# The last block of the first FFN and the whole second FFN go into the planner's order; the first units get an order by hand

## The chip, the cores and the metric

The kernel runs on 1 core of one Trainium2 chip. The metric is the device time of one execution in microseconds (us). Matrix products run on TensorE (PE in the profile; PEld is its weight load), elementwise work on VectorE (DVE), ScalarE (ACT) and GpSimd (POOL), and SyncE (SP) issues all transfers of the program.

## The reference

Attention over a window of 64 positions, an FFN with ELU, and a gated FFN on normalized rows, all in float32 on 2304 tokens of width 512:

```python
scores = scale * np.matmul(q, k.transpose(0, 1, 3, 2))     # 4 batches, 8 heads, 576 positions, head_dim 64
mask = (rel >= 0) & (rel < window)                         # rel = query position - key position, window 64
attn = softmax of np.where(mask, scores, -1e9)
x = np.matmul(attn, v), as 2304 rows of 512

h = x @ w_in                                               # 512 x 2048
x = np.where(h > 0, h, np.exp(np.minimum(h, 0)) - 1) @ w_out   # 2048 x 512

xn = x / np.sqrt(np.mean(x * x, axis=-1) + 1e-6) * rms_g
g = xn @ w_gate                                            # 512 x 1536
out = (g * sigmoid(g) * (xn @ w_val)) @ w_out2             # 1536 x 512
```

## The kernel before

**Precision.** A float32 operand is held as a high part (fp32r) and a low part, and each product is three: high times high, low times high, high times low. A weight tile (a "unit", 128 x 512) goes through four steps: POOL moves the top halves (L569, `s1`), DVE joins the halves (L576, `join`), ACT or DVE makes the high part (L587, `s2`), POOL the low part (L592, `s3`). The text calls these steps G, J, H and L, with the number of the weight, as the new code does. There are 32 such units of the first FFN, all made while block 0 runs; they stay in SBUF as the 32 slots of the tag `wu`.

**First stage.** Tokens go in six blocks of 384. For a block, three attention units of 128 tokens: transpositions of keys and queries (T, L371), scores (S, L403), masking and minimum on DVE (M, L424), exponentials on ACT (E, L430), normalization on DVE (N, L436 to L438), transposition of the weights (TP, L455), values (PV, L467), copies between (L384). Then the first FFN: for each of 16 slices of 128 columns a product `in` (12 matmuls, L621), ELU on ACT and DVE (L669 to L678), and a product `out` two slices later (12 matmuls, L696) into four PSUM banks of the tag `y`. The attention of block b+1 runs between the products of block b. Of each block the four `y` banks are copied to SBUF, normalized and stored in DRAM (`xspill`).

**Second stage.** Three superblocks of 768 tokens. A 2 x 2 Strassen-like scheme needs seven products per pair of column slices instead of eight: weight combinations `pu` are made beforehand by POOL and ACT, stored in DRAM (`pspill`, and `ospill` for the output weights, through two staging tiles `stg`), and loaded again; row combinations X are made by DVE. Each of 6 pairs per superblock has 7 x 12 matmuls (L1022), whose results go through `c` tiles (copies L984 on ACT, sums L988 on DVE), the gate (L993 to L1005), and after three pairs the output product (`outs`, L1056).

**What sets the order.** Class `Plan` (from L25) takes steps with a cost per engine, the tiles they read and write, and for loads a time on the transfer queue (`load`). `run` (L161) repeatedly takes the step that can start first, with `tail` (the longest chain behind it) deciding among those within 0.1 us. `could` (L106) gives the earliest time by engine, inputs and free buffers (`LIMITS`, L22). Costs are raised by `MARGIN`: DVE by 1.2, ACT and POOL by 1.1. Every instruction is then tied behind the one before it on its engine. Before, only blocks 0 to 4 (`planned = nblk - 1`, L1097) are planned. Block 5 and the second FFN are written out at the kernel's end in a fixed interleaving (slots, `after()`), and the order of their instructions on each engine is the scheduler's of the tile framework. There `norm_items` (L705) does the normalization with copies `big<-y` at L708 and the final multiplications at L742; `split_out` (L878) stages output weights (L882, L885).

Of the kernel before, what the change touches and what calls it, by code (L numbers as in the profile page):

```python
# [21 lines left out]
LIMITS = dict(w=4, y=4, wu=32, kT=2, qT=1, ks=1, qs=1, vw=2, s=2, st=3, pT=2, e=2, g=3, x0=1, x1=1,  # L22
# [7 lines left out]
class Plan:  # L30
# [4 lines left out]
    WINDOW, PREFER = 0.1, 0.5  # L35
    MARGIN = {"DVE": 1.2, "ACT": 1.1, "POOL": 1.1}
# [4 lines left out]
    def add(self, costs, fn, reads=(), writes=(), load=0.0, rows=128):  # L41
        x = Step()
        x.costs = {e: c * self.MARGIN.get(e, 1.0) for e, c in costs.items()}
        x.fn, x.index, x.load, x.rows = fn, len(self.steps), load, rows
# [24 lines left out]

    def lag(self, a, e):  # L70
        return 0.0 if a == e else 0.22 if a == "PE" else 0.09

    def tails(self):
# [14 lines left out]
        for t in self.users:  # L88
            if t[0] in LIMITS:
                every.setdefault(t[0], []).append(t)  # L90
                if t[0] not in "wy" and (t[0] != "wu" or t[1][0] in ("r", "in", "out")):
                    self.first.setdefault(t[0], []).append(t)
# [7 lines left out]
        self.queued = {t for ts in self.first.values() for t in ts}  # L100
# [5 lines left out]
    def could(self, x, e):  # L106
        t = self.free.get(e, 0.0)
# [8 lines left out]
        for tag, ts in new.items():  # L116
# [6 lines left out]
            ts = ts.intersection(self.queued)  # L123
            for tile in self.first.get(tag, ()) if ts else ():
                if tile not in self.live:
                    if tile not in ts:
                        return None
                    ts.discard(tile)
                    if not ts:
                        break  # L130
# [30 lines left out]
    def run(self):  # L161
# [10 lines left out]
        ready = [x for x in self.steps if not x.deps]  # L172
        while ready:
            per = {}
# [6 lines left out]
            assert per, ("the plan is stuck", [(list(x.costs), x.tiles, x.index) for x in ready], self.used)  # L181
# [9 lines left out]
            self.put(x, e, t)  # L191
            ready.remove(x)
            for y in after[x.index]:
                wait[y.index] -= 1
                if not wait[y.index]:
                    ready.append(y)
        return self.order


@with_exitstack  # L200
def kernel(
# [99 lines left out]
    N0 = BLOCKS1[0] // 128  # L301
    plan = Plan()
# [27 lines left out]
    def load_steps(nm, i, src, t0, n, bufs):  # L330
# [10 lines left out]
        add({"SP": 0.55 * parts}, go, writes=[a_key(nm, i, bufs)], load=1.25)  # L341
# [10 lines left out]
    def attention(u, xt=None, b=0, x=None):  # L352
# [14 lines left out]
        def turn(bkey, nm):  # L367
# [6 lines left out]
            add({"PE": 0.436}, go, reads=[a_key(nm, u, 1)], writes=[bkey])  # L374
# [11 lines left out]
        turn(bk, "ks")  # L386
        turn(bq, "qs")
# [898 lines left out]
```

## Time and the profile before

| | us |
|---|---|
| median of 3 executions | 933.17 |
| lowest, highest | 933.01, 934.4 |
| the profiled execution | 932.11 |
| its span, first to last instruction | 930.3 |
| PE busy in the span | 905.0 |
| DVE, ACT, POOL busy | 566.8, 446.3, 238.2 |
| mean granted clock of TensorE | 0.994 |

How to read it: the profile is of one execution, so stretches and waits are compared with its own 932.11 us. An engine executes its instructions in order; "idle before" is time in which it had nothing running, with what ended that time behind the arrow. PEclk is the granted share of TensorE's 2.4 GHz: 1.00 or 0.50 (1.2 GHz). A busy PE does not say that it ran at its full clock.

### The profile page before, as it was taken

To read this page: it belongs to the slowest core of one execution; us is meant where nothing else is said; L and a number is where in the kernel's file an instruction comes from. 1 tells how busy PE (TensorE), PEld (TensorE's weight loads), DVE (VectorE), ACT (ScalarE), POOL (GpSimd) and SP (SyncE) were. 2 spreads that over 40 slices of the span, in tenths; PEclk is the share of its full clock that TensorE was granted. 3 is DMA by queue.
4 is the path that set the end of the run, shared out by engine and by line. 5 is a ranking of instruction groups with operands and counts; after the bars stand their busy time and mean duration, and the time that the engine had idled before them with its cause. 6 is when DMAs were issued, how large, how long until landed. Compare 5 with 4: busy or idle time off the path is not lost.

```text
span 930.3 us, 16271 instructions
## 1 busy us (share of the span) xinstructions
PE 905.0 (97%) x5916; PEld 855.7 (92%) x5916; DVE 566.8 (61%) x1266; ACT 446.3 (48%) x1131; POOL 238.2 (26%) x281
## 2 busy tenths in 40 slices
PE   6799999999999999999999999999999999999998
PEld 4798999999999999999999888998998998998996
DVE  5889867567655755674876583375460485460561
ACT  5766565666656566565423642441441441441430
POOL 3687803540561453056123113000000000000000
PEclk9899999999999999999999999999999999999999
DMA  9997117543733663554486487936966747847711
GB/s 210 306 318 207 25 24 216 170 137 101 235 131 103 206 198 118 141 178 160 157 281 240 148 318 249 388 142 236 404 232 213 232 138 268 314 136 252 220 49 69
DMA packets 150401, 182.96 MB, mean 197 GB/s; under 512 B 81712, under 2 KB 111408, under 8 KB 150320
## 3 DMA queue, kind: packets, MB, share of 16 engines
q1 hardware_dynamic: 150320, 181.91, 60.3%
q8 instruction: 47, 0.77, 0.4%
q14 instruction: 34, 0.28, 0.1%
HBM read 144.13 MB, written 37.75 MB: 196 GB/s over the span
## 4 chain that ended last, share of the span: by engine, by line
PE 66%; DMA 12%; DVE 11%; POOL 4%; ACT 4%; issue 2%; SPq 0%; POOLq 0%; ACTq 0%; DVEq 0%
PE y L1022 15%; PE w L1022 11%; PE y L1056 11%; PE w L621 10%; PE y L696 10%; PE w L1056 5%; DMA pspill<-stg 4%; DMA ospill<-stg 3%; DVE wm L576 2%; POOL stg L922 1%; PE w L467 1%; DMA big<-in_moe_w_val_dram 1%; DMA ks<-in_k_dram 1%; DMA big<-in_moe_w_gate_dram 1%; PE w L403 1%
## 5 line engine op out<-in xcount | busy, mean ns | idle before, releaser
L696 PE MATMUL y<-g,wu 128*128 128x384 f32 x1152 | 220.2, 340 | 0.6 <-DVE g L678 0.4
L621 PE MATMUL w<-x,wu 128*128 128x384 f32 x1152 | 217.2, 337 | 0.0
L696 PEld LDWEIGHTS y<-g,wu 128*128 128x128 f32 x1152 | 200.2, 189 | 5.1 <-DVE g L678 1.4
L621 PEld LDWEIGHTS w<-x,wu 128*128 128x128 f32 x1152 | 199.2, 188 | 1.9 <-issue 1.0
L1022 PE MATMUL y<-xw,pu 128*128 128x384 f32 x648 | 123.6, 335 | 1.9 <-ACT big L708 1.3
L1022 PEld LDWEIGHTS y<-xw,pu 128*128 128x128 f32 x648 | 113.3, 188 | 3.2 <-ACT big L708 1.6
L988 DVE TENSOR_TENSOR c<-c,w 128x384 f32<-128x384 f32 x72 | 39.7, 551 | 119.1 <-PE w L1022 118.5
L1056 PE MATMUL y<-wu,g 128*128 128x512 f32 x432 | 106.4, 390 | 0.0
L1056 PEld LDWEIGHTS y<-wu,g 128*128 128x128 f32 x432 | 80.9, 188 | 16.1
L569 POOL CAST top<-big 128x512 f16<-128x512 bf16 x36 | 31.6, 879 | 201.4 <-DMA big<-in_moe_w_gate_dram 63.9
L1022 PE MATMUL w<-xw,pu 128*128 128x384 f32 x432 | 82.6, 334 | 0.0
L1022 PEld LDWEIGHTS w<-xw,pu 128*128 128x128 f32 x432 | 75.6, 188 | 0.1
L678 DVE TENSOR_TENSOR g<-e,g 128x384 fp32r<-128x384 f32 x80 | 59.1, 742 | 20.6 <-ACT g L676 19.5
L673 DVE SCALAR_TENSOR_TENSOR e<-e,w 128x384 f32<-128x384 f32 x80 | 43.6, 549 | 38.7 <-ACT e L671 38.4
L984 ACT COPY c<-y 128x384 f32<-128x384 f32 x72 | 34.4, 481 | 65.7 <-PE y L1022 64.7
L669 ACT ACTIVATE e<-w 128x384 f32<-128x384 f32 x80 | 39.0, 488 | 40.3 <-PE w L621 38.0
L1056 PE MATMUL w<-wu,g 128*128 128x512 f32 x216 | 55.9, 390 | 0.0
L1004 ACT CAST g<-e 128x384 fp32r<-128x384 f32 x69 | 34.9, 512 | 41.5 <-DVE e L998 41.5
L430 ACT ACTIVATE s<-s,st 128x128 f32<-128x128 f32 x120 | 46.7, 391 | 9.2 <-DVE st L424 9.1
L993 ACT ACTIVATE e<-c 128x384 f32<-128x384 f32 x54 | 27.5, 524 | 46.7 <-DVE c L988 46.6
L922 POOL TENSOR_TENSOR stg<-wm,stg 128x256 fp32r<-128x256 f32 x48 | 38.4, 800 | 44.8 <-ACT stg L920 44.7
L1056 PEld LDWEIGHTS w<-wu,g 128*128 128x128 f32 x216 | 40.6, 188 | 8.6
(153 smaller groups left out, 1307.7 us busy)
## 6 DMA issues: line engine op xcount, KB each, us to landing
pu<-pspill SPq DMA_DIRECT2D x126, 512.0 KB, 6.7
pspill<-stg SPq DMA_DIRECT2D x84, 256.0 KB, 2.2
wu<-ospill SPq DMA_DIRECT2D x36, 512.0 KB, 5.9
tmp<-in_moe_w_out_dram SPq DMA_DIRECT2D x16, 511.8 KB, 7.3
tmp<-in_moe_w_in_dram SPq DMA_DIRECT2D x16, 511.0 KB, 7.4
vw<-in_v_dram SPq DMA_DIRECT2D x27, 256.0 KB, 3.7
ospill<-stg SPq DMA_DIRECT2D x24, 256.0 KB, 2.5
big<-in_moe_w_out_dram SPq DMA_DIRECT2D x12, 511.8 KB, 7.5
```

Of the source, the lines that this page charges most:

```text
L430: nc.scalar.activation(out=s_()[:, p, :], in_=s_()[:, p, :], func=AF.Exp, scale=-1.0, bias=st_()[:, 0, p, :], accum_out=st_()[:, 1, p, :])
L621: nc.tensor.matmul(pt[:, :n], lhsT=wt[:, a, kk * 128:(kk + 1) * 128], rhs=xs[kk][:, c, :n], start=(i == 0), stop=(i == len(seq) - 1))
L669: add({"ACT": 0.49}, lambda e: nc.scalar.activation(out=et(), in_=ph(), func=AF.Relu, scale=-1.0), reads=[w], writes=[e_])
L673: add({"DVE": 0.56}, lambda e: nc.vector.scalar_tensor_tensor(out=et(), in0=et(), scalar=-1.0, in1=ph(), op0=ALU.add, op1=ALU.max), reads= ...
L678: add({"DVE": 0.68}, lambda e: nc.vector.tensor_tensor(out=gt()[:, 1, :n], in0=et(), in1=gt()[:, 0, :n].bitcast(F32), op=ALU.subtract), re ...
L696: nc.tensor.matmul(py[m][:, :n], lhsT=wt[:, a, m * 128:(m + 1) * 128], rhs=g[:, c, :n], start=(first and i == 0), stop=(last and i == 2))
L922: add({"POOL": 0.76}, lambda e: nc.gpsimd.tensor_tensor(out=tile_()[:, 1, :], in0=src(), in1=tile_()[:, 0, :].bitcast(F32), op=ALU.subtrac ...
L984: nc.scalar.copy(out=t, in_=bank[b, qi][:, :NB])
L988: nc.vector.tensor_tensor(out=t, in0=t, in1=bank[b, qi][:, :NB], op=ALU.add)
L1004: nc.any.tensor_copy(out=g[:, 0, :], in_=e)
L1022: nc.tensor.matmul(bank[key][:, :NB], lhsT=u[:, qi, a, kk * 128:(kk + 1) * 128], rhs=X[j][kk][:, x, :], start=(first and n == 0), stop=(n ...
L1056: nc.tensor.matmul(po[m], lhsT=g[:, a, (m % 3) * 128:(m % 3 + 1) * 128], rhs=w[:, x, :], start=(first and i == 0), stop=(last and i == 2))
```

## The change

- Block 5 and the second FFN become steps of the plan: `norm_items`, `elu`, `split_out` and the slots of the old end go, and `norm_steps` (with `tail=True` for the last block), `in_steps`, `out_steps`, `put_out`, `x_load`, `x_items`, `p_load`, `o_load`, `pair` and `outs` add steps. The scheduler has no order left to choose.
- The first 20 loads (`LOADS`) and the first steps of units 0 to 2 with weights 0 to 5 (`FIRST`) are placed in an order given by hand; the planner continues from there. H of weights 0 to 4 is put on DVE; before, these five were on ACT. In both programs 27 of the 32 H are on ACT and 5 on DVE.
- A load is planned no earlier than 4 us before the planned end of the transfer queue (`AHEAD`).
- `MARGIN` is now 0.92 for PE and 1 for the others; some costs are other numbers (J 0.85 to 1.05, G 0.88 to 1.0, H on DVE 0.75 to 1.0, N 1.6 in block 1). Keys of unit u are transposed only after the scores of unit u-1.
- The matrix products, their operands and their number are the same.

```diff
-    WINDOW, PREFER = 0.1, 0.5
-    MARGIN = {"DVE": 1.2, "ACT": 1.1, "POOL": 1.1}
+    WINDOW, PREFER, AHEAD = 0.1, 0.5, 4.0
+    MARGIN = {"PE": 0.92}
...
     def could(self, x, e):
-        t = self.free.get(e, 0.0)
+        t = max(self.free.get(e, 0.0), self.dma - self.AHEAD if x.load else 0.0)
...
-    def run(self):
+    def run(self, given=()):
...
+        given = [(x, e) for name, e in given for x in self.steps if x.name == name]
+        pos = 0
         while ready:
+            if pos < len(given):
+                x, e = given[pos]
+                pos += 1
+                e = e if e in x.costs else next(iter(x.costs))
+                self.take(x, e, self.could(x, e), ready, wait, after)
+                continue
...
+    LOADS = "ks0 qs0 ks1 qs1 ks2 qs2 vw0 vw1 w0 vw2 vw3 w1 vw4 vw5 w2 w3 w4 w5 w6 w7"
+    FIRST = (
+        "Tk0 Tq0 CK0 CKa0 Tk1 CQ0 S0 CK1 Tq1 M00 E00 Tk2 CKb0 M01 CQ1 N00 CK2 S1 E01 CKb1 TP00 "
...
-    for b in range(planned):
-        n = BLOCKS1[b]
+    for b in range(nblk):
+        n, last = BLOCKS1[b], b == nblk - 1
+        slots = {}
...
+        if last:
+            x_load(0)
+            for j in range(AHEAD2):
+                slots.setdefault(7 + j, []).append(lambda n=j: p_load(0, n))
+            for j in range(F2 // 2):
+                slots.setdefault(6 + j * 10 // (F2 // 2), []).append(lambda j=j: prep_out(j))
+            for j, fn in enumerate(x_items(0)):
+                slots.setdefault(7 + j * 3 // 2, []).append(fn)
...
-    def norm_steps(b, n, tok0):
+    def norm_steps(b, n, tok0, tail=False):
...
...
+        def keep(pos, qi, j):
+            ck, bk = c_key(pos, qi), bank(j, qi)
+            add({"ACT": 0.48}, lambda e: nc.scalar.copy(out=c_of(ck), in_=at(bk)),
+                reads=[bk], writes=[ck])
...
-    for x, e in plan.run():
+    for x, e in plan.run(given):
```

**Where instructions move.** First, SP at the program's start (tmp tiles of keys, queries and values of units 0 to 2 by their DRAM tensors; `in_moe_w` are weights of the first FFN). Before:

```order
L293 DMA tmp_135<-in_k_dram 128x8x64
L293 DMA tmp_137<-in_q_dram 128x8x64
L293 DMA tmp_139<-in_v_dram 64x8x64 x2
L293 DMA tmp_139<-in_v_dram 128x8x64
L293 DMA tmp_135<-in_k_dram 128x8x64
L293 DMA tmp_137<-in_q_dram 128x8x64
L293 DMA tmp_150<-in_v_dram 128x8x64 x2
L293 DMA tmp_163<-in_k_dram 128x8x64
L293 DMA tmp_167<-in_q_dram 128x8x64
L563 DMA tmp_187<-in_moe_w_in_dram 128x4x511
L563 DMA tmp_189<-in_moe_w_in_dram 128x4x511
L293 DMA tmp_194<-in_v_dram 128x8x64 x2
```

After the change:

```order
L307 DMA tmp_135<-in_k_dram 128x8x64
L307 DMA tmp_137<-in_q_dram 128x8x64
L307 DMA tmp_135<-in_k_dram 128x8x64
L307 DMA tmp_137<-in_q_dram 128x8x64
L307 DMA tmp_141<-in_k_dram 128x8x64
L307 DMA tmp_143<-in_q_dram 128x8x64
L307 DMA tmp_145<-in_v_dram 64x8x64 x2
L307 DMA tmp_145<-in_v_dram 128x8x64
L586 DMA tmp_149<-in_moe_w_in_dram 128x4x511
L307 DMA tmp_151<-in_v_dram 128x8x64 x2
L586 DMA tmp_154<-in_moe_w_in_dram 128x4x511
L307 DMA tmp_156<-in_v_dram 128x8x64 x2
```

Keys and queries of all three units now stand ahead of the first values, the first weight ahead of the values of units 1 and 2, and the second weight behind those of unit 1.

Second, ACT at the end of block 5, where its `y` banks are copied (`big<-y`, L708 before, L738 now); `stg<-wm` are staging copies of output weights, `c<-y` the first copies of the second FFN, `x<-xb` row combinations. Before:

```order
L882 CAST stg<-wm 128x256 x2
L841 CAST x_6159<-xb 128x384
L639 ACTIVATE e<-w 128x384
L841 CAST x_6165<-xb 128x384
L882 CAST stg<-wm 128x256
L640 ACTIVATE e<-e 128x384
L882 CAST stg<-wm 128x256 x3
L708 COPY big_6170<-y 128x384
L708 COPY big_6171<-y 128x384
L712 ACTIVATE big_6172<-big_6170 128x384 x2
L882 CAST stg<-wm 128x256 x2
```

After the change:

```order
L863 CAST stg<-wm 128x256
L685 CAST g<-e 128x384
L863 CAST stg<-wm 128x256
L678 ACTIVATE e<-w 128x384
L680 ACTIVATE e<-e 128x384
L821 CAST x_6101<-xb 128x384
L821 CAST x_6122<-xb 128x384 x2
L685 CAST g<-e 128x384
L863 CAST stg<-wm 128x256 x2
L738 COPY big_6163<-y 128x384 x2
L738 COPY big_6175<-y 128x384
```

Before, three staging copies in a row stand right in front of the bank copies, of which ACT does two; now two stand there, and ACT does three of the four.

Third, DVE in the first three pairs, where the normalization of block 5 ends with its multiplications by `g_sb` (L742 before, L763 now), among the sums `c<-c,w` (L988, now L987) that free PSUM banks. Before:

```order
L737 SCALAR_TENSOR_TENSOR big_6172<-e,big_6172 128x384
L998 TENSOR_TENSOR e<-e,y 128x384
L988 TENSOR_TENSOR c<-c,w 128x384
L742 SCALAR_TENSOR_TENSOR big_6170<-big_6170,g_sb,big_6172 128x384 x2
L742 SCALAR_TENSOR_TENSOR big_6171<-big_6171,g_sb,big_6172 128x384 x2
L988 TENSOR_TENSOR c<-c,w 128x384
L1005 TENSOR_TENSOR g<-e,g 128x384
L994 TENSOR_TENSOR e<-e,c 128x384
L988 TENSOR_TENSOR c<-c,y 128x384 x2
L988 TENSOR_TENSOR c<-c,w 128x384
```

After the change:

```order
L759 SCALAR_TENSOR_TENSOR big_6242<-e,big_6242 128x384
L987 TENSOR_TENSOR c<-c,w 128x384
L763 SCALAR_TENSOR_TENSOR big_6163<-big_6163,g_sb,big_6242 128x384
L987 TENSOR_TENSOR c<-c,w 128x384
L991 TENSOR_TENSOR e<-e,c 128x384
L987 TENSOR_TENSOR c<-c,y 128x384 x2
L991 TENSOR_TENSOR e<-e,c 128x384
L987 TENSOR_TENSOR c<-c,w 128x384
L991 TENSOR_TENSOR e<-e,c 128x384
L987 TENSOR_TENSOR c<-c,w 128x384
```

The four multiplications stood together ahead of a sum; now one stands between two sums, and none of the other three among the next seven rows.

## Rows read from the trace of the kernel before

**Rows 1.** The page, part 1: busy time, share of the span, instructions.
```profile
PE 905.0 (97%) x5916; PEld 855.7 (92%) x5916; DVE 566.8 (61%) x1266; ACT 446.3 (48%) x1131; POOL 238.2 (26%) x281
```

**Rows 2.** Busy time by stage: stretch, length, engines' busy us, PEclk, DMA share, GB/s.
```profile
32.80:43.05 10.25, 7.71 (x52) 7.10 (x44) 9.34 (x30) 7.71 (x26) 9.40 (x9) 1.00 1.02 269
43.05:46.46 3.41, 3.22 (x13) 3.23 (x13) 2.79 (x5) 2.01 (x4) 1.21 (x3) 0.50 1.04 362
46.46:120.00 73.54, 72.14 (x573) 68.65 (x572) 65.14 (x122) 44.61 (x111) 59.50 (x49) 1.00 0.61 174
120.00:500.00 380.00, 377.99 (x2800) 365.41 (x2799) 246.61 (x603) 221.68 (x602) 135.72 (x167) 1.00 0.54 167
500.00:538.00 38.00, 36.01 (x202) 34.47 (x201) 25.27 (x49) 18.01 (x41) 7.79 (x10) 1.00 0.39 126
538.00:541.40 3.40, 1.46 (x9) 1.14 (x7) 3.40 (x8) 0.13 (x1) 0.00 (x0) 1.00 0.69 170
541.40:544.80 3.40, 3.19 (x10) 3.19 (x11) 3.23 (x8) 1.85 (x4) 0.00 (x0) 0.50 1.00 378
560.00:920.00 360.00, 360.00 (x1887) 335.68 (x1885) 174.09 (x339) 121.49 (x255) 8.14 (x11) 1.00 0.63 222
```

**Rows 3.** Timeline of ACT, 9 to 34 us: start, length, instruction, idle before.
```profile
9.84 0.40 ACT L430 ACTIVATE tmp<-tmp,st 128x128 f32<-128x128 f32 x1 [2.54 <-DVE st L424]
...
31.22 0.65 ACT L481 CAST x<-w 128x256 fp32r<-128x256 f32 x2 [1.50 <-PE w L467]
```

**Rows 4.** Groups of ACT, 4 to 34 us: count, busy us, mean ns, idle before.
```profile
L430 ACT ACTIVATE tmp<-tmp,st 128x128 f32<-128x128 f32 x24 | 9.3, 390 | 4.7 <-DVE st L424 4.7
...
L384 ACT COPY tmp<-y 128x512 f32<-128x512 f32 x5 | 2.8, 583 | 0.0
```

**Rows 5.** Timeline of DVE, 26 to 28 us.
```profile
26.67 0.22 DVE L436 TENSOR_SCALAR st<-st 128x4 f32<-128x4 f32 x1 [0.43 <-ACT tmp L430]
...
27.14 0.69 DVE L438 TENSOR_TENSOR tmp<-tmp,st 128x512 f32<-128x512 f32 x1
```

**Rows 6.** Timeline of PE, 31 to 46 us.
```profile
31.11 1.91 PE L403 MATMUL w<-kT,qT 64*64 64x128 f32 x32
32.95 6.52 PE L621 MATMUL w<-x,wu 128*128 128x384 f32 x36
39.31 0.60 PE L455 MATMUL w<-ident,s 128*128 128x128 f32 x4
42.45 0.63 PE L371 MATMUL w<-ident,ks 128*128 128x128 f32 x4 [2.54 <-DMA ks<-in_k_dram]
```

**Rows 7.** Groups of all engines, 33 to 113 us (block 0).
```profile
L592 POOL TENSOR_TENSOR wu<-wm,wu 128x512 fp32r<-128x512 f32 x29 | 42.9, 1500 | 2.5 <-ACT wu L587 2.0 <-DVE wu L587 0.4
...
L576 DVE SCALAR_TENSOR_TENSOR wm<-tmp,big 128x512 int32<-128x512 int32 x27 | 28.2, 1064 | 2.6 <-POOL wu L592 1.9 <-POOL big L569 0.7
...
L438 DVE TENSOR_TENSOR s<-s,st 128x512 f32<-128x512 f32 x6 | 5.8, 975 | 0.2
...
L587 DVE CAST wu<-wm 128x512 fp32r<-128x512 f32 x5 | 5.1, 1021 | 0.1
...
L436 DVE TENSOR_SCALAR st<-st 128x4 f32<-128x4 f32 x6 | 4.5, 748 | 0.6 <-ACT s L430 0.6
```

**Rows 8.** Timeline of PE, 500 to 546 us.
```profile
515.51 3.40 PE L1022 MATMUL y<-xw,pu 128*128 128x384 f32 x18 [1.30 <-ACT big L708]
519.51 2.67 PE L1022 MATMUL y<-xw,pu 128*128 128x384 f32 x12 [0.60 <-ACT c L984]
...
541.61 3.81 PE L1022 MATMUL y<-x,pu 128*128 128x384 f32 x12 [2.15 <-DVE c L988]
```

**Rows 9.** Timeline of ACT, 500 to 546 us.
```profile
514.03 0.40 ACT L882 CAST stg<-wm 128x256 fp32r<-128x256 f32 x1 [7.88 <-DMA ospill<-stg]
```

**Rows 10.** Timeline of DVE, 500 to 546 us.
```profile
537.49 2.20 DVE L742 SCALAR_TENSOR_TENSOR big<-big,g_sb,big 128x384 f32<-128x384 f32 x4
```

**Rows 11.** DMA issues: KB each, median us to landing.
```profile
pu<-pspill SPq DMA_DIRECT2D x126, 512.0 KB, 6.7
```

More of the change, by code (lines that the diff above doesn't have):

```diff
@@ L90, in tails @@
                 every.setdefault(t[0], []).append(t)
-                if t[0] not in "wy" and (t[0] != "wu" or t[1][0] in ("r", "in", "out")):
-                    self.first.setdefault(t[0], []).append(t)
+                if self.queue(t):
+                    self.first.setdefault(self.queue(t), []).append(t)
         for tag, ts in every.items():
@@ L122, in could @@
                 t = max(t, f[need - 1] + 0.1)
[L123 to L126, printed above, removed]
-                        return None
-                    ts.discard(tile)
-                    if not ts:
-                        break
+            for tile in ts:
+                for other in self.first.get(self.queue(tile), ()):
+                    if other == tile:
+                        break
+                    if other not in self.live and other not in ts:
+                        return None
         return t
@@ L180, in run @@
                         per.setdefault(e, []).append((t, -self.tail[x.index], x.index))
-            assert per, ("the plan is stuck", [(list(x.costs), x.tiles, x.index) for x in ready], self.used)
+            assert per, "the plan is stuck"
             best = None
@@ L190, in run, with take @@
             (t, _), x, e = best
[L191 to L196, printed above, removed]
-        return self.order
+            self.take(x, e, t, ready, wait, after)
+        return self.order
+    def take(self, x, e, t, ready, wait, after):
+        self.put(x, e, t)
+        ready.remove(x)
+        for y in after[x.index]:
+            wait[y.index] -= 1
+            if not wait[y.index]:
+                ready.append(y)
 @with_exitstack
@@ L942, in prep_steps @@
[L942 removed]
+        put(3, both, sk)
+        put(4, q4[1, 1], k4[1, 1])
     def prep_out(j):
[L946 to L958 removed]
@@ L1086 @@
     fwp = Feeder(w2src, big4, None, 2)
-    prep_o = [fn for j in range(F2) for fn in prep_out(j)]
     top = []
@@ L1096 @@
     nblk = len(BLOCKS1)
-    planned = nblk - 1
-    at_f = {0: (4, 9, 14)}
     for u in range(N0):
@@ L1254 @@
                 fn()
+    given = [(nm, "SP") for nm in LOADS.split()]
+    for nm in FIRST.split():
+        op = nm.rstrip("0123456789")
+        given.append((nm, "DVE" if op in ("CKa", "CKb", "H") else "ACT"))
+    before = {}
+    for x, e in plan.run(given):
+        done = len(nc.cur_bb.bb.instructions)
+        x.fn(e)
+        for i in nc.cur_bb.bb.instructions[done:]:
+            if i.engine in before:
+                tc.add_manual_dep(
+                    i, before[i.engine],
+                    mybir.DependencyInfo(
+                        mybir.DependencyClass.NoSync, mybir.DependencyReason.DATA),
+                    reason="order")
+            before[i.engine] = i.name
 _INS = ['q', 'k', 'v', 'moe_w_in', 'moe_w_out', 'moe2_w_gate', 'moe2_w_val', 'moe2_w_out',
```

591 lines of the change are left out of this document (272 added, 319 removed), and 3 rows, old and new, of the table FIRST.

## The prediction

> **What bounds the kernel now.** I read the page's busy shares first: PE is busy 905.0 of the 930.3 us span, 97%, and DVE, ACT and POOL stay at 61% or below [rows 1]. The change leaves every product as it is, so it can only win from PE's gaps, from its slow clock, and from the way those are passed on. At most 25.3 us lie in gaps.
>
> Second, busy time by stage says where the gaps are. From 46.46 to 120 us PE misses 1.40 us, from 120 to 500 another 2.01, from 560 to 920 nothing: 360.00 of 360.00 [rows 2]. What is left lies at two places. One is the start: PE has 7.71 of 10.25 us before 43.05, and the stretch behind it has a granted clock of 0.50, the lower of the two levels, for 3.22 busy us, so about 1.6 us are lost there [rows 2]. The other is the handoff from the first FFN to the second, 500 to 545 us: 1.99 and 1.94 us of gaps, 0.21 more, and 3.19 busy us at clock 0.50, again about 1.6 us lost [rows 2]. The handoff costs 1.99 + 1.94 + 0.21 + 1.6 = 5.74 us.
>
> Third, PE's timeline names who is late. At the start the first `in` product runs at 32.95, then PE waits 2.54 us for the keys of unit 4 [rows 6]. In the handoff it waits 1.30 us for the copies of the `y` banks, 0.60 for a `c` copy, both on ACT, and 2.15 for a `c` sum on DVE [rows 8]. Behind the first is a queue: ACT stood 7.88 us at a staging copy whose buffer an `ospill` still read [rows 9], and the bank copies are right behind it in ACT's order. Behind the third, DVE ran four multiplications of the normalization in one go, 2.20 us [rows 10], and the sum that frees a PSUM bank came after them. After the wait of 2.15 us the clock was 0.50; after the 2.54 us too. So a gap of two us costs nearly four here.
>
> **The start, step by step.** SP now brings keys and queries of units 0 to 2 first. The two loads of unit 0, which the first transposition waits for, stay first, so PE's start is not moved. PE then does one more transposition ahead of the first scores; one of four matmuls takes 0.60 to 0.63 us [rows 6], so the first exponential comes at about 9.84 + 0.5 = 10.3 [rows 3]. From there ACT is the chain: 24 exponentials of 0.39 us are 9.3 us [rows 4], and the new order puts five copies of 0.58 us among them, 2.9. The last exponential ends at 10.3 + 9.3 + 2.9 = 22.5. In the program before, the last normalization only begins at 26.67 [rows 5].
>
> Then DVE. J and H of weight 0 now stand right in front of that last normalization. J took 1.06 us on average and H on DVE 1.02 while POOL worked [rows 7]; together about 2.1 us, of which the exponentials cover about one, so they end near 23.5. The normalization took 27.14 + 0.69 - 26.67 = 1.16 us with POOL not at L [rows 5]; in block 0 its two large parts took 0.75 and 0.98 [rows 7], so up to 2.0 us with the rest. It ends between 24.7 and 25.5; I take the later value, because POOL starts on weights just then.
>
> From that end (27.14 + 0.69 = 27.83 before, [rows 5]) to the first product the trace has 32.95 - 27.83 = 5.12 us, but 32.95 - 31.11 = 1.84 of it are the scores of unit 3 [rows 6], which now come later: 3.28. The casts of x, 0.65 us [rows 3], hid behind those scores and are now bare. The first product starts at 25.5 + 3.28 + 0.65 = 29.4 instead of 32.95.
>
> That lead is not the gain. The loads ahead of the keys of unit 4 are the same in both orders, eleven weights among them, so these keys land at about 42.4 again. The gain is what PE has done more at that point. Up to there the new order has four `in` products, one `out`, the scores and two transpositions of unit 3. A product of 12 matmuls takes 6.52 / 3 = 2.17 us [rows 6], so this is 10.9 + 1.8 + 1.3 = 14.0, from 29.4 to 43.4, and about a microsecond less if the matmuls of the small steps overlap. PE then no longer waits. Before, it had done three `in` and one transposition of weights (0.60) by then. The lead is two products less 0.60, 3.7 us, less up to 0.95 if PE arrives at 43.4 rather than 42.45. To this comes the slow clock, 1.6 us, since the wait ahead of it goes. So 4.4 to 5.3; **I take 5.0**. The cases outside: nothing at all, if the weights are late; and 8, if PE is never short of work and also starts warm.
>
> **Block 0 to block 5: 0.** The rest of block 0 is packed. Between 46.46 and 120 us DVE is busy 65.14 of 73.54 and POOL 59.50 [rows 2], and 29 steps L of 1.50 us are 42.9 of it [rows 7]. There is no room to win more than the 3.41 us of gaps from 46.46 to 500. The planner's costs are now bare (no margin on DVE, ACT and POOL), so a step that is later than planned moves its followers; at the end of block 0 attention also stands bare before the next block's products. I bound this by 2 us of loss beyond one gap, some 3 in all. Between -3.4 and +3 nothing pulls the value to either side: 0.
>
> **The handoff: 5.4.** ACT now does three of the four bank copies and still has two staging copies in front of them. But staging now begins earlier against the queue, each x load and `ospill` is placed by its planned time, and the four multiplications no longer stand ahead of a sum. With one of 2.20 / 4 = 0.55 us ahead of the sum [rows 10], the wait of 2.15 loses 3 x 0.55 = 1.65, which leaves 0.5. A gap that short I take as keeping the clock up, so the 1.6 come back as well. The waits on ACT go if the planner knows the `ospill`'s end. Everything gone would be 5.7, nothing 0; I take 5.4, nearer the full value, because each of the three waits is one the planner has costs for.
>
> **The second FFN: 0.** PE is at 360.00 of 360.00 us [rows 2], so nothing is to be won. Its cover is DVE at 174 us busy of 360, and loads of the weight combinations, 126 transfers of 512 KB that land in 6.7 us [rows 11]. The order by plan costs nothing as long as no sum or load is late. If one is, a case like 541.61 is repeated.
>
> **Sum.** -5.0 + 0 - 5.4 + 0 = -10.4: 932.11 - 10.4 = 921.7 for an execution like the profiled one. The median lies 1.06 above that, so **922.8**. With all bounds on the good side (8 + 3.4 + 5.7) it is 916.1; with 2 us less at the start, 3 lost in the middle and 1 lost in the handoff 928.8.
>
> **Rivals.** *B: block 0 is bound by preparing weights, and the start's lead is given back.* PE begins earlier but POOL and DVE make weights no faster. For it: L rose to 1.50 us in block 0, H on DVE costs 1.02, and the small step of a normalization rose to 0.75 us [rows 7] from 0.22 [rows 5]. Five H are on DVE in both programs, but now they are the first five, on the path to the first products. If each meets one L of 1.50, that is 7.5 us, more than the 5.0. Against it: from 46 us on PE is short by only 1.40 us in block 0. The time is then 932.11 - 5.4 + 1.06 = 927.8.
>
> The Trainium skill, page "SBUF — State Buffer", section "Who interferes with whom", says that DVE copies and casts in their two-port mode, and DVE operations with two SBUF inputs, share a port pair with GpSimd, and that whoever issues first blocks the other fully. By that rule the five casts alone would give rival B. The trace agrees on the direction, with the 0.75 beside 0.22, and does not show who blocks whom.
>
> *C: the handoff's waits stay.* ACT still meets `ospill` at the staging copies, the bank copies still stand behind two of them, and the 7.88 us [rows 9] are only moved. Then only the start is won: 932.11 - 5.0 + 1.06 = 928.2. If B and C hold together, nothing is left: 933.2.
>
> *D: slower, by new waits on DVE in the second FFN.* The planner ties every sum in a fixed place, with true costs instead of raised ones. Where a gate step or a multiplication is put ahead of a sum that frees a bank, PE waits as at 541.61: 2.15 us, and 1.6 for the clock behind it, 3.75 each. Two cost 7.5 and leave it faster; from the third (11.3 against 10.4) it is slower, 934.1; four give 937.8. For it: DVE works in bursts there, 3.40 of 3.40 us before the one wait [rows 2]. Against it: 360 us in a row without a gap at a DVE load of 48%, from an order that only a fixed interleaving gave.
>
> That the change does not do what it says is excluded: each instruction is tied behind the one ahead on its engine, and the order of the program shows the moves.
>
> **How the numbers follow.** Forecast 0.62, B 0.14, C 0.08, B with C 0.06, D 0.10. A measurement of this kernel can tell 0.2%, 1.9 us, from no change. Faster are the forecast, B and C, 0.84; same is B with C, 0.06; slower D, 0.10. The range takes in the forecast with its bounds, B and C with up to 3 us lost in the middle, 916 to 931; it leaves out B with C, and D.
>
> **What would show it.** Right: first `in` near 29.4; no wait for keys near 42 and no clock of 0.50 there; no wait above 1 us in the handoff; PE without gaps in the second FFN. Wrong: a first `in` after 32, or more than 3.4 us of gaps between 46 and 120 us (rival B); ACT still standing at `ospill` with PE behind it (C); waits of PE for `c` or for `pu`, with a clock of 0.50 behind them, in the last 380 us (D).

## The result and the profile after

| us | before | after |
|---|---|---|
| median of 4 executions | 933.09 | 918.03 |
| lowest, highest | 929.19, 934.4 | 916.61, 918.64 |
| the profiled execution | 932.11 | 918.25 |
| its span | 930.3 | 916.5 |

The ratio is 0.9843, interval 0.9812 to 0.9875: 15 us less, between 11.7 and 17.5. Faster was forecast at 922.8, range 916 to 931. The changed program lies in the range, 4.8 us below the forecast. The median of before is from four executions here; in the four groups of 9 to 29 executions further below it is 929.77 to 931.83, and the changed program, timed once more beside it (e5), won 12.6 us by the ratio, between 10.9 and 14.3.

Busy time by stage after the change, the stretches of [rows 2], with one more ahead of them and the last one ending at 912 us (busy us of PE, PEld, DVE, ACT, POOL with their counts, then PEclk, DMA share, GB/s):

```profile
24.93:28.34 3.41, 2.94 (x53) 2.76 (x50) 3.38 (x7) 1.42 (x5) 2.67 (x2) 0.50 1.03 372
32.80:43.05 10.25, 8.98 (x80) 8.07 (x79) 9.33 (x29) 8.25 (x28) 7.94 (x8) 1.00 1.12 288
43.05:46.46 3.41, 3.41 (x27) 3.37 (x25) 1.70 (x4) 2.65 (x8) 2.40 (x2) 1.00 1.06 379
46.46:120.00 73.54, 71.94 (x602) 68.28 (x601) 65.98 (x125) 53.20 (x138) 57.16 (x47) 1.00 0.65 182
120.00:500.00 380.00, 379.29 (x2783) 368.21 (x2782) 243.11 (x573) 229.21 (x612) 132.88 (x166) 1.00 0.52 163
500.00:538.00 38.00, 36.69 (x211) 36.10 (x210) 27.27 (x51) 22.90 (x50) 6.90 (x9) 1.00 0.71 256
538.00:541.40 3.40, 3.40 (x21) 3.40 (x21) 2.49 (x6) 1.15 (x3) 0.00 (x0) 1.00 0.00 0
541.40:544.80 3.40, 3.40 (x22) 3.40 (x21) 2.88 (x6) 1.35 (x3) 0.00 (x0) 1.00 0.86 257
560.00:912.00 352.00, 352.00 (x1849) 328.92 (x1848) 174.60 (x335) 123.15 (x259) 12.43 (x15) 1.00 0.67 233
```

The clock of 0.50 is gone from both places of [rows 2] where it stood, and 538 to 544.8 us have no gap. One stretch at 0.50 is left near the start, 24.93 to 28.34. Before had one there too, which [rows 2] leave out; this is the row of before:

```profile
29.40:32.80 3.40, 3.40 (x62) 3.18 (x62) 2.73 (x6) 1.90 (x6) 1.47 (x3) 0.50 1.04 378
```

So of three such stretches two are gone and one stays. PE's timeline after, the lines that answer to [rows 6] and [rows 8]:

```profile
28.07 4.55 PE L647 MATMUL w<-x,wu 128*128 128x384 f32 x24 [0.47 <-ACT x L504]
...
33.65 0.63 PE L391 MATMUL w<-ident,qs 128*128 128x128 f32 x4 [0.49 <-DMA qs<-in_q_dram]
35.05 2.36 PE L647 MATMUL w<-x,wu 128*128 128x384 f32 x12 [0.78 <-DVE e L682]
37.34 1.10 PE L424 MATMUL w<-kT,qT 64*64 64x128 f32 x32
...
42.66 0.60 PE L391 MATMUL w<-ident,ks 128*128 128x128 f32 x4
...
515.91 0.91 PE L745 MATMUL w<-big,ones 128*128 128x384 f32 x2 [1.31 <-DVE big L733]
```

The first product runs at 28.07 instead of 32.95, and the keys of unit 4 are no longer waited for. One wait is left in the handoff, 1.31 us for the sum of squares of the normalization. ACT after, just ahead of the copies of the `y` banks ([rows 9] before):

```profile
495.66 0.41 ACT L863 CAST stg<-wm 128x256 fp32r<-128x256 f32 x1 [2.81 <-DMA ospill<-stg]
...
500.59 0.86 ACT L738 COPY big<-y 128x384 f32<-128x384 f32 x2 [0.38 <-PE y L705]
```

ACT still waits for `ospill`, but the bank copies now wait for PE, not PE for them.

**Where the time came from.** Gaps alone do not tell it, since PE can be busy at a low clock. So all matmuls of a trace were added up in order, each with its usual interval (0.173 us for one of 384 columns, and so on, 886 us in all), and it was noted when PE came to the same amount of work in each program. The difference is the lead over the profiled execution of before. The intervals of the small matmuls are uncertain, so single values hold to about 0.3 us. In the table "work 30" is reached by before at 53.0 us, 120 at 145.9 (block 0 done), 475 at 506.6, 530 at 569.0.

```
lead over the profiled execution of before, us
work of PE, us            30     120     475     530     886
after                    5.4     5.0     7.6    13.1    13.4
after, once more (e5)    4.4     4.2     7.7    14.8    15.1
e4 no hand order         5.0    -0.5     2.9     9.8    10.1
e6 loads only            3.5     0.9     4.5    11.3    11.6
e7 H on ACT              3.2     2.2     5.7    11.3    11.7
e8 old factors           0.0    -6.5    -4.5     0.9     1.3
e9 N ahead of J, H       1.5     2.6     5.3    12.0    12.3
e10 all factors 1        3.9     2.8    -3.0     2.6     3.0
e11 no load limit        2.3     0.2     3.6    10.5    10.8
e12 N and x ahead        4.1     3.9     7.2    13.7    14.0
e1 (order of before)     0.3     0.3    -0.6     3.1     3.1
e2 (order of before)     0.4     0.4     0.5     2.4     2.4
e3 (order of before)    -0.8    -0.8     0.2     4.4     3.9
```

After: 5.4 at the start, -0.4 in the rest of block 0, 2.6 up to the handoff, 5.5 in it, 0.3 in the second FFN. For e8 the point 475 falls on a wait of 1.20 us of PE; just ahead of it its lead is -3.0.

### The profile page after: what moved, and what is told of

Its sections match the earlier page's. It is cut to its first block, busy times and chain, and to the rows that moved or that the text cites. A ratio compares the mean times of both kernels' runs of the same rounds, so it can differ in the third digit from the quotient of the medians.

```text
span 916.5 us, 16241 instructions
## 1 busy us (share of the span) xinstructions
PE 895.6 (98%) x5916; PEld 850.3 (93%) x5916; DVE 562.1 (61%) x1228; ACT 464.0 (51%) x1169; POOL 238.9 (26%) x281
## 4 chain that ended last, share of the span: by engine, by line
PE 88%; DVE 4%; DMA 3%; issue 2%; POOL 1%; ACT 1%; SPq 0%; ACTq 0%; POOLq 0%; DVEq 0%
PE w L647 20%; PE y L705 19%; PE y L1024 16%; PE w L1024 12%; PE y L1066 11%; PE w L1066 5%; PE w L490 2%; PE w L424 2%; DVE wm L599 2%; PE w L477 1%; DMA ospill<-stg 1%; PE w L391 1%; DMA big<-in_moe_w_val_dram 1%; DMA tmp<-in_k_dram 1%; PE w L745 0%
## 5 line engine op out<-in xcount | busy, mean ns | idle before, releaser
L705 PE MATMUL y<-g,wu 128*128 128x384 f32 x1152 | 217.2, 337 | 1.3 <-DVE g L687 1.3
L987 DVE TENSOR_TENSOR c<-c,w 128x384 f32<-128x384 f32 x72 | 39.7, 553 | 130.3 <-PE w L1024 125.5
L1066 PE MATMUL y<-wu,g 128*128 128x512 f32 x432 | 103.0, 390 | 0.0
L865 POOL TENSOR_TENSOR stg<-wm,stg 128x256 fp32r<-128x256 f32 x72 | 58.9, 823 | 118.0 <-ACT stg L863 117.8
L682 DVE SCALAR_TENSOR_TENSOR e<-e,w 128x384 f32<-128x384 f32 x96 | 52.5, 549 | 60.4 <-ACT e L680 60.4
L678 ACT ACTIVATE e<-w 128x384 f32<-128x384 f32 x96 | 47.0, 490 | 82.7 <-PE w L647 79.8
L687 DVE TENSOR_TENSOR g<-e,g 128x384 fp32r<-128x384 f32 x96 | 69.5, 726 | 21.9 <-ACT g L685 19.9
L592 POOL CAST top<-big 128x512 f16<-128x512 bf16 x36 | 28.8, 800 | 145.5 <-DMA big<-in_moe_w_out_dram 60.1
L991 DVE TENSOR_TENSOR e<-e,c 128x384 f32<-128x384 f32 x108 | 59.3, 563 | 1.3 <-ACT e L1002 0.8
L685 ACT CAST g<-e 128x384 fp32r<-128x384 f32 x87 | 44.4, 512 | 20.1 <-DVE e L682 19.9
L599 DVE SCALAR_TENSOR_TENSOR wm<-big,top 128x512 int32<-128x512 int32 x36 | 27.9, 774 | 41.0 <-POOL stg L865 28.6
```

Source lines behind the costliest of these rows:

```text
L599: nc.vector.scalar_tensor_tensor(out=m.bitcast(I32), in0=self.r.pop(i).bitcast(I32).rearrange("p (f t) -> p f t", t=2)[:, :, 0], scalar=13 ...
L678: add({"ACT": 0.49}, lambda e: nc.scalar.activation(out=et(), in_=ph(), func=AF.Relu, scale=-1.0), reads=[w], writes=[e_])
L682: add({"DVE": 0.56}, lambda e: nc.vector.scalar_tensor_tensor(out=et(), in0=et(), scalar=-1.0, in1=ph(), op0=ALU.add, op1=ALU.max), reads= ...
L685: add({"ACT": 0.52, "DVE": 0.42}, lambda e: copy_on(e)(out=gt()[:, 0, :n], in_=et()), reads=[e_], writes=[(*g_, "h")])
L687: add({"DVE": 0.68 if b else 0.93}, lambda e: nc.vector.tensor_tensor(out=gt()[:, 1, :n], in0=et(), in1=gt()[:, 0, :n].bitcast(F32), op=AL ...
L705: nc.tensor.matmul(py[m][:, :n], lhsT=wt[:, a, m * 128:(m + 1) * 128], rhs=g[:, c, :n], start=(first and i == 0), stop=(last and i == 2))
```

## The experiments

Each run was timed beside the program before on the same chip. That program's median was 929.77, 930.67, 931.83 and 930.8 us in the four groups (e1 to e4, e5 to e8, e9 to e11, e12).

**e1, the multiplications spread, in the program before.** They get four slots of their own instead of two, and extra dependencies keep them there on DVE:

```diff
...
-                put(i, fn)
+                put(i if i < 8 else (15, 17, 18, 19)[i - 8], fn)
```

> The program before, with one thing of the change alone: the four multiplications that end the last normalization no longer stand in one piece ahead of a c sum; one stands there, the other three come later among the sums. Theory (a sum that waits behind four multiplications stops PE, and the stop costs the low clock too): the PE wait of 2.15 us near 541.6 falls to about 0.5, the 3.2 busy us at clock 0.50 behind it are gone, 3.2 to 3.7 us are won, about 929 against 932.5. Rival (PE would have to wait there anyway, for a load or for ACT): a wait of 1.5 us or more stays with the clock at 0.50, within 1 us of before. A third case: the wait goes, but the clock falls all the same, 1.6 to 2.1 us won.

928.27 us, ratio 0.9973 (0.9959 to 0.9987): 2.5 us won by the ratio, between 1.2 and 3.8; the medians lie 1.5 apart. PE's timeline of this run:

```profile
515.56 3.41 PE L1030 MATMUL y<-xw,pu 128*128 128x384 f32 x18 [1.09 <-ACT big L708]
...
540.05 2.35 PE L1030 MATMUL y<-x,pu 128*128 128x384 f32 x12 [0.55 <-DVE c L996]
```

The wait of 2.15 is 0.55, and from 538 to 545 us the clock is 1.00. PE comes to the place at the same time as before (539.51 against 539.46); what moved is the sum on DVE, here before and then in this run:

```profile
541.01 1.01 DVE L988 TENSOR_TENSOR c<-c,y 128x384 f32<-128x384 f32 x2
```

```profile
539.45 1.01 DVE L996 TENSOR_TENSOR c<-c,y 128x384 f32<-128x384 f32 x2
```

The theory holds in the trace, where the lead grows by 3.7 us in the handoff (-0.6 to 3.1); the timed executions show rather less than the 3.2 to 3.7.

**e2, bank copies on DVE, in the program before.**

```diff
-            (nc.any if m % 2 else nc.vector).tensor_copy(out=y[m], in_=py[m][:, :n])
+            (nc.any if m % 2 and not tail else nc.vector).tensor_copy(out=y[m], in_=py[m][:, :n])
```

> The program before, with all four y banks of the last block copied by DVE, so that no bank copy stands behind the staging copies that wait for ospill on ACT. Theory (ACT's queue behind ospill makes the waits of 1.30 and 0.60 us): the first goes, the second may stay because c copies still stand on ACT behind staging; 1.0 to 1.9 us won. Rival (the wait moves whole to the c copies behind the same staging copies): under 0.4 us won, with a PE wait of more than 1.2 us on ACT c near 517.

930.59 us, ratio 1.0005 (0.9989 to 1.002): nothing. The rival holds. PE's timeline:

```profile
518.63 3.42 PE L1022 MATMUL y<-xw,pu 128*128 128x384 f32 x12 [2.11 <-ACT c L984]
...
540.72 2.36 PE L1022 MATMUL y<-x,pu 128*128 128x384 f32 x12 [0.50 <-DVE c L988]
```

The wait went over to the `c` copies behind the same staging copies and became longer, 2.11 against 1.30 and 0.60. ACT's timeline:

```profile
516.64 0.41 ACT L882 CAST stg<-wm 128x256 fp32r<-128x256 f32 x1 [1.59 <-DMA ospill<-stg]
...
518.12 0.46 ACT L984 COPY c<-y 128x384 f32<-128x384 f32 x1
```

Behind the wait of 2.11 the clock is 0.50, from 520.27 to 523.68 us. The second line of PE is worth a look: the four multiplications are still in one piece here, yet PE waits only 0.50, with the clock at 1.00 behind it. PE comes there 0.76 us later than before (540.22 against 539.46), and the sum on DVE 0.89 us earlier (540.12 against 541.01); together this is the whole difference from 2.15. So that wait is not a fixed price of the four multiplications: a wait ahead of it on PE's path shortens it.

**e3, both edits.**

> The program before with both edits together: multiplications spread, bank copies on DVE. Theory (the two causes are separate and make the whole handoff gain): 4.5 to 5.6 us won, as much as the last 5.4 us of the lead that the changed program builds between 500 and 545 us. Rival (one cause hides the other, or the planned order of the block itself is needed): no more than the larger of the two single gains, 3.7 us or less.

928.99 us, ratio 0.9991 (0.9977 to 1.0005): at most 2.1 us won, so the rival's bound. In the trace PE waits 1.40 us for `c` on ACT and 0.54 for the sum, and its lead in the handoff is 4.2 us, far more than the timed executions show. Moving the bank copies does not cure ACT's part; e2 and e3 point to the staging copies as the cause, but no run moved those in the program before.

**e4, the change without the order by hand.**

```diff
-    for x, e in plan.run(given):
+    for x, e in plan.run():
```

> The changed program without the order by hand: neither the 20 loads nor the first steps are given, the planner chooses them with its new costs and load limit. Theory (the start's lead of 5.3 us comes from the hand order): first in product near 33 again, a wait for the keys of unit 4 with clock 0.50 behind it, time about 923, 4.5 to 6 us above the changed program. Rival (the new costs and the load limit would have found it alone): first in product before 31, time within 2 us of the changed program, 917 to 920.

922.38 us, ratio 0.9916 (0.9898 to 0.9934). The time is the theory's, the way is not. The first product runs at 30.39, as the rival had it, and the lead at work 30 is 5.0. It is lost in block 0. PE's timeline, then busy time by stage:

```profile
84.27 0.63 PE L477 MATMUL w<-ident,s 128*128 128x128 f32 x4 [1.91 <-DVE s L460]
```

```profile
86.00:92.00 6.00, 6.00 (x50) 5.88 (x47) 6.00 (x5) 3.87 (x8) 6.00 (x5) 0.75 0.59 134
```

PE waits for a normalization, and the clock falls behind it, while DVE and POOL are both busy without a break. This is rival B of the prediction, in a neighbour of the change. So the order by hand does not make the start's lead; it keeps it through block 0.

**e5, the changed program once more.**

> The changed program once more, unchanged, beside the next three on the same chip, as their yardstick. 916.5 to 919.5 us; the lead over the profiled execution of before, counted in PE's work done, should again be about 5.3 us at 48 us, 7 to 8 at 480 and 13 to 13.5 from 530 on. If the leads come out otherwise by more than 1 us, the split into start, middle and handoff is not a property of the program.

917.53 us, ratio 0.9865 (0.9846 to 0.9883). At work 30 and 120 the leads are 1.0 and 0.8 smaller than in the first execution, at 475 the same. The handoff gives 7.1 here instead of 5.5: no wait is left between 500 and 560 us, the 1.31 for L745 included. That is more than the 1 us that was allowed for, so the handoff's share is known to about 1.6 us only.

**e6, only the loads by hand.**

```diff
-    for nm in FIRST.split():
+    for nm in ():
```

> The changed program with the 20 loads given by hand, but the first steps of PE, ACT, DVE and POOL left to the planner. Without both, the lead at 48 us was 5.0 and was lost again by 84 us in block 0, where PE waited 0.67 and 1.91 us with a low clock behind it; the run took 922.4. Theory (what keeps the lead through block 0 is that the keys, queries and weights come in the order given): no wait above 1 us between 70 and 100, within 1.5 us of the changed program. Rival (the steps by hand, with weights 0 to 4 made early, keep it): a PE wait of 1 us or more between 60 and 100 us, 3 us or more above the changed program.

921.22 us, ratio 0.9904 (0.9889 to 0.992), 3.7 above e5. The time is the rival's, the wait that it named is not: between 60 and 100 us none is above 0.73. The long one comes earlier, and the lead at work 120 is 0.9. PE's timeline:

```profile
47.59 1.06 PE L477 MATMUL w<-ident,s 128*128 128x128 f32 x8 [2.47 <-DVE e L682]
...
82.41 0.33 PE L490 MATMUL w<-pT,vw 128*64 128x64 f32 x2 [0.73 <-ACT pT L405]
...
100.58 0.97 PE L705 MATMUL y<-g,wu 128*128 128x384 f32 x4 [0.85 <-DVE g L687]
```

Behind the wait of 2.47 us the clock stays at 1.00 (46.46 to 80 us).

**e7, H of weights 0 to 4 on ACT.**

```diff
-        given.append((nm, "DVE" if op in ("CKa", "CKb", "H") else "ACT"))
+        given.append((nm, "DVE" if op in ("CKa", "CKb") else "ACT"))
```

> The changed program with H of weights 0 to 4 on ACT instead of DVE in the hand order. Theory (DVE is the engine that is short in block 0, 65 of 73 us busy, and ACT has room there): first product within 0.5 us of 28.1, time within 1 us of the changed program or up to 2 us better. Rival (on ACT the five casts of 0.62 us stand in the chain of exponentials that sets the first product): first product 1 to 3 us later, up to 3 us above. A third case, by the Trainium skill, page SBUF — State Buffer, section Who interferes with whom (DVE casts and POOL's reads lock each other out): the five L behind these H become faster, from 1.3 to 1.5 us towards 1.1 or less.

920.29 us, ratio 0.9888 (0.9873 to 0.9904), 2.8 above e5. The rival holds. PE's and ACT's timelines:

```profile
29.34 6.01 PE L647 MATMUL w<-x,wu 128*128 128x384 f32 x24 [2.12 <-ACT x L504]
```

```profile
27.86 0.62 ACT L610 CAST wu<-wm 128x512 fp32r<-128x512 f32 x1 [1.82 <-DVE wm L599]
28.38 0.64 ACT L504 CAST x<-y 128x256 fp32r<-128x256 f32 x2
28.91 0.66 ACT L504 CAST x<-w 128x256 fp32r<-128x256 f32 x2
```

H of weight 2 waits on ACT for its J, and the casts of x, due earlier, stand behind it. The third case fell: the first three L took 1.71, 1.28 and 1.28 us, against 1.26, 1.66 and 1.27 in the changed program. The long one of either run begins while a J, not an H, runs on DVE (last section).

**e8, the old factors on the costs.** PE's factor is back at 1 here too:

```diff
-    MARGIN = {"PE": 0.92}
+    MARGIN = {"DVE": 1.2, "ACT": 1.1, "POOL": 1.1}
```

> The changed program with the old factors on the planner's costs (DVE 1.2, ACT and POOL 1.1, PE as it is), the order by hand kept. Theory (bare costs and PE's 0.92 make the gain of 2.4 us between 48 and 480 us): lead at 48 us as in the changed program, 1.5 to 3 us less of it at 480, time 1.5 to 4 us above. Rival (the middle's gain comes from the load limit and the new rules, not from the factors): within 1 us at 480 us. The handoff should keep its 5 us by either.

931.06 us, ratio 1.0004 (0.9992 to 1.0017). The whole gain is gone, and not where the theory looked. From work 120 on the lead still grows, by 3.5 us up to the wait at 475 and by 3.9 from there through the handoff. What is lost is the start and block 0: the lead is 0.0 at work 30 and -6.5 at 120. Busy time by stage:

```profile
46.46:80.00 33.54, 31.09 (x286) 29.16 (x285) 25.56 (x64) 23.86 (x68) 23.22 (x20) 1.00 1.06 323
80.00:120.00 40.00, 37.06 (x295) 34.61 (x293) 34.62 (x56) 25.93 (x64) 32.20 (x27) 1.00 0.23 52
```

From 46.46 to 80 us DVE does 25.56 us of work (30.00 in e5) and POOL 23.22 (30.02 in e5): the plan that takes them for slower than they are leaves them idle where they are short. That the raised costs do this, and not PE's factor, follows with e10, which also has PE at 1 and keeps a lead of 2.8 at work 120. Which of the three factors it is was not tried: against PE, ACT and POOL stand at 1.1 here and at 1 / 0.92 = 1.09 in the change, DVE at 1.2; and no factor touches the times of loads.

**e9, one normalization ahead.** The planned order, with N of the last half unit moved ahead of J and H of weight 0 on DVE:

```diff
-    for x, e in plan.run(given):
+    order = plan.run(given)
+    names = [x.name for x, e in order]
+    n21 = order.pop(names.index("N21"))
+    order.insert(max(i for i, s in enumerate(names) if s == "E21") + 1, n21)
...
```

> The changed program with one step moved on DVE and nothing else: the last normalization of the first units stands ahead of J and H of weight 0 instead of behind them. In the changed program its multiplication took 1.57 us beside L of weight 0 on POOL (21.85 to 23.11), against 0.69 alone, and PE waited 2.06 us for it. Theory (DVE was held by POOL's L, and the chain to the first product ends there): the multiplication takes 0.7, PE's wait falls below 1 us, the first product comes about 1.5 us earlier, near 26.6, and 0.5 to 1.5 us are won. Rival (the next thing is late, weight 0 or the keys and queries of the next units): the first product comes earlier but the time stays within 0.4 us.

917.43 us, ratio 0.9848 (0.9831 to 0.9866): not to be told from e5 (917.53, 0.9846 to 0.9883, on another chip). The multiplication took 0.69 us and the first product came at 26.40, as the theory had it; then a new wait took it all, with the clock at 0.50 from 30.06 to 36.89 us. PE's timeline:

```profile
26.40 1.66 PE L647 MATMUL w<-x,wu 128*128 128x384 f32 x8 [0.47 <-ACT x L504]
...
30.78 5.49 PE L647 MATMUL w<-x,wu 128*128 128x384 f32 x16 [2.73 <-DVE x L508]
```

The low parts of x (L508) stand behind J and H of weight 2 on DVE. The rival holds, with another late thing than it named.

**e10, all factors 1.**

```diff
-    MARGIN = {"PE": 0.92}
+    MARGIN = {}
```

> The changed program with all factors on the planner's costs at 1, PE's too (0.92 in the change). The old factors took the whole gain away, 9.6 us of it before 120 us. Theory (the raised costs of DVE, ACT and POOL did that): with only PE's factor back at 1 the time stays within 2 us of the changed program, and the lead at 120 us is 3 us or more. Rival (PE's 0.92 did it: a plan that thinks PE slower makes weights later): 5 us or more above the changed program, lead at 120 us near or below 0.

929.63 us, ratio 0.9982 (0.9968 to 0.9997). The time is the rival's, the lead at work 120 (2.8) nearly the theory's: the 5.8 us are lost between 120 and 475. PE's timeline there, then ACT's ahead of the second of these waits:

```profile
163.36 1.10 PE L424 MATMUL w<-kT,qT 64*64 64x128 f32 x32 [1.22 <-ACT qT L405]
245.38 1.10 PE L424 MATMUL w<-kT,qT 64*64 64x128 f32 x32 [1.81 <-ACT qT L405]
328.60 1.10 PE L424 MATMUL w<-kT,qT 64*64 64x128 f32 x32 [1.46 <-ACT qT L405]
411.15 1.10 PE L424 MATMUL w<-kT,qT 64*64 64x128 f32 x32 [2.32 <-DVE qT L405]
```

```profile
242.34 0.41 ACT L863 CAST stg<-wm 128x256 fp32r<-128x256 f32 x1 [0.91 <-DMA pspill<-stg]
...
244.73 0.59 ACT L405 COPY qT<-w 128x512 f32<-128x512 f32 x1
```

Once per block the scores wait for a copy, three times on ACT, where it stands behind staging copies that wait for the store of the staging buffer, and once on DVE. Behind the wait of 1.81 the clock is 0.50, from 246.52 to 249.93 us. The factor of 0.92 makes the plan think that PE comes 8% earlier than it does, so such copies are placed early enough. In e8, with PE at 1 as well but the others raised, PE has no wait between 140 and 500 us.

**e11, no limit on loads.**

```diff
-    WINDOW, PREFER, AHEAD = 0.1, 0.5, 4.0
+    WINDOW, PREFER, AHEAD = 0.1, 0.5, 1000.0
```

> The changed program without the limit on loads (4 us ahead of the queue becomes 1000). In its order the keys and queries of unit 4 come behind more than 20 weight loads instead of eleven. Theory (the limit keeps the loads of block 1's attention in time): attention of block 1 comes late, the lead at 120 us falls by 3 us or more, or a wait of 1 us or more for it stands near the end of block 0. Rival (with the first loads given by hand the limit decides nothing): within 1 us of the changed program. For the stretch from 120 to 475 us, where every plan with the new rules so far won 2 to 3.5 us over before: if the limit made that gain, less than 1 us of it is left here; if the other new rules did, 2 us or more.

920.67 us, ratio 0.9887 (0.9869 to 0.9905), 3.2 above e9. The lead at work 120 is 0.2, as in the theory. From 120 to 475 it grows by 3.4, so the limit did not make that gain.

**e12, e9's new wait taken away.** N21 behind E21 as in e9, and J, H and L of weight 2 behind the low parts of x:

```diff
...
+    for name, behind in (("N21", "E21"), ("J2", "XL2"), ("H2", "J2"), ("L2", "H2")):
+        move(name, behind)
...
```

> As the run before with the last normalization moved ahead, and J, H and L of weight 2 moved behind the low parts of x as well, since those low parts stopped PE for 2.73 us in that run. Theory (both DVE waits of the start can be taken away): first product near 26.5, no wait of 1 us or more for the low parts of x, no low clock before 46 us, lead at 120 us of 5.5 to 7, time 0.5 to 1.5 us below the changed program's 917.5. Rival (the next late thing takes it: keys and queries of unit 3, which landed at about 33.6 in the changed program, or the weights): PE waits 1 us or more for one of these before 46 us and the time stays within 0.4 us of the changed program.

917.7 us, ratio 0.9857 (0.9834 to 0.9881): again not to be told from e5. PE's timeline:

```profile
26.70 4.58 PE L647 MATMUL w<-x,wu 128*128 128x384 f32 x24 [0.47 <-ACT x L504]
...
32.18 0.66 PE L391 MATMUL w<-ident,ks 128*128 128x128 f32 x4 [0.90 <-DMA ks<-in_k_dram]
33.30 0.63 PE L391 MATMUL w<-ident,qs 128*128 128x128 f32 x4 [0.46 <-DMA qs<-in_q_dram]
```

The wait for x is gone, and PE now stands at the keys and queries of unit 3. The granted clock from 32.8 to 46.46 us is 0.88. The rival holds by the time and by what PE waits for, though the two waits are 0.90 and 0.46 us and neither is the whole us that it named. Neither e9 nor e12 shows a gain over the changed program.

## Why the prediction was right

**The start, 5.0 forecast, 5.4 measured (5.4 and 4.4 in two executions).** The term held, and its main argument too: PE reaches the keys of unit 4 at 42.66 (43.4 forecast), without a wait and at clock 1.00, with just the work done that was listed: four `in` products, one `out`, the scores and two transpositions of unit 3. These keys had landed at 42.31 before, at 41.24 after and at 42.31 in e5, so they are a fixed point to about 1 us. The first product was forecast at 29.4 and came at 28.07. This 1.3 us made no difference, since PE then waited 0.49 and 0.78 us on the way, 1.27 in all, where the forecast had no wait.

Two sizes on the way were off. ACT's chain was too long: the first exponential came at 9.33, not 10.3, and the last ended at 20.99, not 22.5. And the scores of unit 3 were taken at 1.84 us from a row of the stretch 29.40 to 32.80, which ran at clock 0.50; at 1.00 they took 1.10. ACT's timeline after:

```profile
9.33 0.40 ACT L452 ACTIVATE tmp<-tmp,st 128x128 f32<-128x128 f32 x1 [1.03 <-DVE st L446]
...
20.58 0.41 ACT L452 ACTIVATE tmp<-tmp,st 128x128 f32<-128x128 f32 x1
```

The step between was right: the normalization was held by POOL (below), its multiplication took 1.57 us, and it took 1.97 from 21.68 on where up to 2.0 was forecast. From its end to the first product it took 4.42, not 3.93; the stretch at clock 0.50 lies in there. The traces of e1 to e3, whose order up to there is that of before, have the first product at 33.47, 30.73 and 32.05, and the keys of unit 4 at 42.19, 41.98 and 42.59. In the order of before the first product of one execution is a poor measure, and PE's start on those keys a good one.

**Block 0 to block 5, 0 forecast, 2.2 measured** (-0.4 to the end of block 0, +2.6 from there to the handoff; 3.3 in all in e5). This step failed, within its bounds of -3.4 to 3. I took it that bare costs would give no slack where the raised ones had. The change puts the slack on PE instead: e10, without it, loses 5.8 us in this stretch. The load limit is not the source (e11). With the old factors e8 still gains 3.5 from work 120 to its wait at 475, no less than the changed program. So slack of either kind keeps this stretch free of waits, and the 2.6 over before, which had the old factors too, probably come from rules that were not tried one by one (keys after scores, the order of tiles in a ring); which of them stays open.

**The handoff, 5.4 forecast, 5.5 measured (7.1 in e5).** The size held, against the one execution that it was read from. Of its causes e1 shows one: with the multiplications spread, the wait and the low clock went. For the ACT waits I named the right queue, but e2 shows that moving the bank copies away gains nothing; the `c` copies behind the staging are late then. The sign "no wait above 1 us" failed in the first execution, by the 1.31 for L745, and held in e5. One thing stays open. The 5.74 us come from one execution of before. The trace of e2 is 1.9 us ahead of it in the handoff (0.5 to 2.4) though e2's time is that of before; in e3 the trace gains 4.2 us there and the ratio at most 2.1. So an average execution of before probably loses less than 5.74 in the handoff; how much was not measured, and the hit of 5.5 on 5.4 is in part owed to the common yardstick. Nor is a wait of 2 us always worth nearly 4: the 2.47 us of e6 had no stretch at 0.50 behind it, while the 1.73 us that e1 waits for the keys of unit 4 had one, from 43.37 to 46.78. What is sure is that the changed program has hardly a wait in the handoff.

**The second FFN, 0 forecast, 0.3 measured.** PE is busy 352.00 of 352.00 us from 560 to 912, at clock 1.00. No new wait: rival D did not come.

**The sum.** Forecast 10.4, lead measured 13.4, profiled executions 13.9 apart. Of the 4.8 us between 922.8 and 918.03 the middle is 2.2, which is the step that was mis-sized most, and the start 0.4. The forecast put the median of after 1.06 above its profiled execution, as before had it, and it lies 0.2 below; this makes 1.3. The rest is spread thin.

**Rivals.** B was real, though not in the changed program. e4, e6, e8 and e11 each give back 2 to 6.5 us between work 30 and 120, and e4 does so by a wait for DVE as B had it. Its price by five L of 1.50 was not how it came: e7 takes the five H from DVE and is slower. C did not come.

## What to carry to other kernels

Give a planner true costs for the engines that are short, and put its slack on the engine that must not wait, by planning it a few per cent faster than it is; here the old factors took back the whole gain by the end of block 0, and no factor at all took most of it in the blocks after. Find the fixed point of a start, a load whose landing the change does not move, and count the work done by then, not the time of the first product: in e9 and e12 the first product came 1.4 to 1.7 us sooner and nothing was won. When one wait is removed, look on the same path for the next: in these two and in e2 it left no gain that could be measured. Before pricing a gap from one profile, look at a second execution: here the wait of 2.15 us of before is 0.50 in e2 with the same four multiplications in one piece. And read the length of a product only where the clock is known: the same 32 scores took 1.91 us at 0.50 and 1.10 at 1.00.

## What was not expected of the hardware

A cast on DVE and a multiplication on DVE take very different times beside POOL. The changed program, DVE's timeline, and POOL's:

```profile
21.33 0.43 DVE L610 CAST wu<-wm 128x512 fp32r<-128x512 f32 x1
...
22.08 1.57 DVE L460 TENSOR_TENSOR tmp<-tmp,st 128x512 f32<-128x512 f32 x1
...
25.15 0.68 DVE L599 SCALAR_TENSOR_TENSOR wm<-tmp,big 128x512 int32<-128x512 int32 x1
25.87 1.38 DVE L610 CAST wu<-wm 128x512 fp32r<-128x512 f32 x1
```

```profile
21.85 1.26 POOL L615 TENSOR_TENSOR wu<-wm,wu 128x512 fp32r<-128x512 f32 x1 [1.63 <-DVE st L458]
...
25.31 1.66 POOL L615 TENSOR_TENSOR wu<-wm,wu 128x512 fp32r<-128x512 f32 x1 [1.03 <-DVE wu L610]
```

The cast takes 0.43 us alone and 1.38 when it comes after an L has begun, and ends 0.28 us behind that L (27.25 against 26.97). The multiplication takes 1.57 and ends 0.54 behind its L; in e9, where POOL is idle, it takes 0.69:

```profile
22.45 0.69 DVE L460 TENSOR_TENSOR tmp<-tmp,st 128x512 f32<-128x512 f32 x1
```

It goes the other way too: the L of 25.31 began while the J of 25.15 ran on DVE and took 1.66 us, the L of 21.85 began ahead of the multiplication and took 1.26. In e7 the L of 1.71 began at 23.65, with a J on DVE from 23.54 to 24.23. The mean of 1.02 for a cast, on which the prediction rested, is a mix: the five in block 0 of before take 0.43 to 1.40. The Trainium skill, page "SBUF — State Buffer", section "Who interferes with whom", says that whoever issues first holds the shared port pair for the whole instruction; these rows agree, and e9 shows that moving one DVE step out of an L's way frees it.
